# A Trainium2 attention and experts kernel: tiles of x handed back at another place, softplus with ScalarE's exponential, another order of v's loads, and stores issued by ScalarE

## The chip, the core and the metric

The program runs on one core of one Trainium2 chip. A core has five engines with instruction queues of their own: TensorE (PE; its weight loads PEld stand apart in the profile), VectorE (DVE), ScalarE (ACT), GpSimd (POOL) and SyncE (SP). Each runs its queue in order, and they wait for each other through semaphores. The metric is device time in microseconds of one execution, lower is better.

## The reference

Three stages follow one another. Attention over q, k, v of shape (4, 8, 576, 64) adds a local one (a band of 3 positions to either side) and one over means of 4 positions, repeated 4 times. Its output, as x with 2304 rows of 512, goes through a mixture of 8 experts with two experts for each row, and then through one with a single expert for each row.

```python
out = repeat(softmax(q_d @ k_d.T * scale) @ v_d, 4) + softmax(where(|i - j| < 4, q @ k.T * scale, -1e9)) @ v
x = out.transpose(0, 2, 1, 3).reshape(2304, 512)

noisy = x @ w_gate + log1p(exp(x @ w_noise)) * noise
top2, weight = two largest of noisy, softmax over these two
x = sum over the two of weight * relu(x @ w1[e]) @ w2[e]

e = argmax(x @ gate2 + modality_bias[modality_id]),  w = its softmax value
x = w * relu(x @ w1_2[e]) @ w2_2[e]
```

The log1p(exp(.)) over the noise logits is the softplus that the change touches.

## The kernel before

**The attention loop.** Heads go in pairs, 16 of them (4 batches of 4 pairs); two pairs are a group g, whose q, k and v are loaded together. The loop over i from 0 to 17 is software-pipelined. Step i begins with the transposes of q and k of pair i + 1 (`transposes`, tiles pq and pk), finishes the softmax of pair i - 1 (`softmax2`: VectorE's sum sm and reciprocal, then the banded probabilities Pd, three quarters on GpSimd, and the coarse ones ped on GpSimd), and multiplies pair i - 2 with v (`values`, tiles pva and pvm; `scale_d` copies od). Then come the scores of pair i (`scores`, tile pd), the output of pair i - 2 into xT (`combine`), the transposes of pair i - 1's probabilities (`p_transposes`: pp, copied to pT by ScalarE, then ppd, copied to pdT), the first half of pair i's softmax (`softmax1`: mx, pe and an exponential; `softmax_d1` and `softmax_d2`: mxd, ped, smd), and on even steps the rest of the next group (`group`, tile prs). `pool_v` adds four rows of v (vr) into vd on GpSimd, six additions for a group.

**Tiles of x.** x has 18 tiles of 128 rows. `xback_att(t)` multiplies xT of one tile with gw (an identity beside the gates' weights), which gives the rows of x and their logits in one PSUM tile px, from the pool of the scores' tiles (two buffers). Its second half, `rest`, waits in the list `after` until `flush()` is called: ScalarE copies the rows to xr (two buffers), VectorE reduces the logits to lg, and SyncE stores xr to x_rows in HBM. Tiles 0 to 12 are placed in the loop by the tables `before` (ahead of a step's scores) and `behind` (after its coarse transposes); tiles 13 to 17 follow the loop.

**Routing inside the loop.** `route1` is a generator for the routing of the first nine tiles: softplus, the two largest, ranks (`rt.places`, L504 to L507), then 18 pairs of one-hot matrices, oh on VectorE and ol on GpSimd, which TensorE multiplies (`rt.invert`, L551) into a table tab; from it `places_early` makes the indices of the gather. `tick(n)` takes n pieces from it, so that routing instructions stand between those of the softmax; a piece that yields "PE" waits for `unblock`. `route1` is put into `back` in step 12. It is used again for the other nine tiles while the experts run.

**SyncE's queue.** Loads and stores are issued in program order: `load_qk(g + 2)` and `load_vr(g + 1)` in odd steps, `load_vw(g)` in even ones, a store for each tile of x, and in step 14 the first weights (raw) and 5.9 MB of zeros into the rows of the second stage. A DMA whose buffer isn't free holds up all that stand behind it.

**Experts.** After the loop the rows are gathered by indirect DMA (xg), transposed (L729), and multiplied with w1 and w2 split in two parts each (L746, L758), until the end.

## Time and profile before

| | |
|---|---|
| median of 3 runs | 925.9 us (923.14 to 927.91) |
| profiled execution, its own time | 926.93 us |
| its span in the trace | 925.2 us |
| mean granted TensorE clock | 0.973 |
| TensorE busy | 870.4 us (94%), 6775 matmuls |
| VectorE, ScalarE, GpSimd busy | 550.4, 429.0, 322.3 us |
| attention and first routing | 0 to about 178 us |
| first matmul of the experts | 177.83 us |

The busy shares are means over two very different parts: up to about 178 us several engines pass work around in a loop, and behind it TensorE works almost without a gap. The page's slices of the span show both: TensorE has 5 to 9 tenths in the first eight slices, and 9 in nearly all that follow. A timeline row gives the start, the duration, the engine, the line and operation, the names, how many like instructions were merged, and in brackets the idle time of the engine just before, with what ended it. SyncE's rows are the time of issuing a DMA, waits of later merged ones included.

### The profile page before, as it was taken

What the parts mean: (1) busy time and instruction counts of PE and PEld (TensorE: products, weight loads), DVE (VectorE), ACT (ScalarE), POOL (GpSimd) and SP (SyncE); (2) the same over time, 40 slices, a digit from 0 to 9 for tenths busy, and PEclk for the clock granted to TensorE, in tenths of its full rate; (3) what the DMA queues carried; (4) which work ended last, traced back from release to release, by engine and by line L of the source; (5) the groups of instructions that cost most, each with busy time, mean ns of one, the idle gap of its engine ahead of it and who ended that gap; (6) DMA issues with size and microseconds to landing.
All of it is one profiled execution on the core that took longest, in us unless ns stands there. A gap on an engine that the chain in (4) does not pass through costs nothing. (4 is left out here: it accounts for less than half of the span.)

```text
span 925.2 us, 18236 instructions
## 1 busy us (share of the span) xinstructions
PE 870.4 (94%) x6775; PEld 764.1 (83%) x6775; DVE 550.4 (59%) x1345; ACT 429.0 (46%) x947; POOL 322.3 (35%) x460
## 2 busy tenths in 40 slices
PE   5898977799999999999999999989989999999995
PEld 4777866698888988999898999978867889999994
DVE  6775697489975544554343443434666877556662
ACT  3675644455554534444233342334423356455552
POOL 7876658436553213043106032050020442222210
PEclk9998988899999999999999999999989999999998
DMA  8878659747776457476328245175433467546650
GB/s 175 171 159 189 169 143 329 240 167 229 204 235 195 140 146 181 143 204 147 129 71 182 92 92 162 46 161 161 128 99 109 155 239 245 190 154 220 216 209 24
DMA packets 158702, 153.83 MB, mean 166 GB/s; under 512 B 74319, under 2 KB 119887, under 8 KB 158608
## 3 DMA queue, kind: packets, MB, share of 16 engines
q1 hardware_dynamic: 146528, 120.15, 42.2%
q0 software_dynamic: 12080, 32.45, 15.2%
q8 instruction: 56, 0.92, 0.4%
q14 instruction: 38, 0.31, 0.1%
HBM read 124.98 MB, written 27.85 MB: 165 GB/s over the span
## 5 line engine op out<-in xcount | busy, mean ns | idle before, releaser
L746 PE MATMUL ph<-xh,whi 128*128 128x256 f32 (+3 forms) x768 | 238.4, 310 | 2.8 <-DVE wlo L707 2.1
L746 PE MATMUL ph<-xl,whi 128*128 128x256 f32 (+3 forms) x768 | 237.6, 309 | 0.4 <-DVE xl L732 0.3
L746 PE MATMUL ph<-xh,wlo 128*128 128x256 f32 (+3 forms) x768 | 237.6, 309 | 0.1
L758 PE MATMUL y<-whi,hh 128*128 128x512 f32 x472 | 192.2, 407 | 0.1
L758 PE MATMUL y<-wlo,hh 128*128 128x512 f32 x472 | 188.1, 398 | 0.0
L758 PE MATMUL y<-whi,hl 128*128 128x512 f32 x472 | 187.6, 398 | 0.0
L707 DVE TENSOR_TENSOR wlo<-raw,whi 128x512 fp32r<-128x512 f32 x135 | 93.2, 690 | 157.4 <-ACT whi L706 144.9
L706 ACT ACTIVATE whi<-raw 128x512 fp32r<-128x512 f32 x160 | 101.0, 631 | 170.7 <-PE y L758 155.7
L746 PEld LDWEIGHTS ph<-xh,whi 128*128 128x128 f32 x768 | 146.0, 190 | 12.2 <-issue 2.6
L746 PEld LDWEIGHTS ph<-xl,whi 128*128 128x128 f32 x768 | 145.9, 190 | 8.3 <-DVE xl L732 1.0
L748 ACT ACTIVATE hh<-ph 128x256 fp32r<-128x256 f32 (+3 forms) x192 | 83.2, 433 | 142.3 <-PE ph L746 133.0
L746 PEld LDWEIGHTS ph<-xh,wlo 128*128 128x128 f32 x768 | 146.2, 190 | 1.8 <-DVE wlo L707 0.3
L749 DVE SCALAR_TENSOR_TENSOR hl<-ph,hh 128x256 fp32r<-128x256 f32 (+3 forms) x192 | 92.5, 482 | 84.5 <-ACT hh L748 81.0
L1215 POOL DMA_INDIRECT x_rows<-y,idx x35 | 57.4, 1641 | 208.1 <-ACT y L1206 108.2
L709 DVE TENSOR_TENSOR wlo<-raw,whi 128x512 fp32r<-128x512 f32 x160 | 120.6, 754 | 11.9 <-ACT whi L708 10.9
L758 PEld LDWEIGHTS y<-whi,hl 128*128 128x128 f32 x472 | 89.5, 190 | 21.6 <-DVE hl L749 0.4
L758 PEld LDWEIGHTS y<-whi,hh 128*128 128x128 f32 x472 | 90.2, 191 | 13.6 <-DVE y L1208 0.8
L758 PEld LDWEIGHTS y<-wlo,hh 128*128 128x128 f32 x472 | 89.8, 190 | 12.6
L708 ACT ACTIVATE whi<-raw 128x512 fp32r<-128x512 f32 x160 | 98.6, 616 | 0.0
L732 DVE TENSOR_TENSOR xl<-pt,xh 128x512 fp32r<-128x512 f32 x59 | 38.7, 687 | 30.8 <-ACT xh L731 30.6
L271 POOL TENSOR_TENSOR Pd<-pe,sm 32x380 f32<-32x380 f32 (+1 forms) x48 | 42.1, 877 | 42.8 <-ACT kT L198 10.4
L1215 POOL DMA_INDIRECT out_dram<-y,pi x19 | 20.6, 1084 | 100.6 <-ACT y L1206 44.1
(311 smaller groups left out, 1085.5 us busy)
## 6 DMA issues: line engine op xcount, KB each, us to landing
raw<-in_moe_w_dram SPq DMA_DIRECT2D x160, 512.0 KB
x_rows<-zero SPq DMA_DIRECT2D x1, 5934.0 KB
vr<-in_v_dram SPq DMA_DIRECT2D x16, 288.0 KB
x_rows<-xr SPq DMA_DIRECT2D x18, 256.0 KB
x2l<-x_rows SPq DMA_DIRECT2D x18, 256.0 KB
qk<-in_q_dram SPq DMA_DIRECT2D x32, 128.0 KB
qk<-in_k_dram SPq DMA_DIRECT2D x32, 128.0 KB
vw<-in_v_dram SPq DMA_DIRECT2D x24, 128.0 KB
```

The source lines that it names most:

```text
L271: eng.tensor_tensor(Pd[s, :, W * g:W * g + n], pe[s, :, :n], sm[s, :, None].to_broadcast([W, 2 * NB, n]), op=ALU.mult)
L706: nc.scalar.activation(h1, a, AF.Copy)
L707: eng.tensor_tensor(l1, a, h1.bitcast(F32), op=ALU.subtract)
L708: nc.scalar.activation(hi[:, 1], r2[:, half], AF.Copy)
L709: nc.vector.tensor_tensor(lo[:, 1], r2[:, half], hi[:, 1].bitcast(F32), op=ALU.subtract)
L732: nc.vector.tensor_tensor(xl, p, xh.bitcast(F32), op=ALU.subtract)
L746: nc.tensor.matmul(ps, w[a][:, k], x[b][:, k, s], start=(i == 0), stop=(i == 3 * KD - 1))
L748: nc.scalar.activation(hh[:, s], ps, AF.Relu)
L749: nc.vector.scalar_tensor_tensor(hl[:, s], ps, 0.0, hh[:, s].bitcast(F32), op0=ALU.max, op1=ALU.subtract)
L758: nc.tensor.matmul(p, h[a][:, 128 * j:128 * j + 128], w[b], start=(f == 0 and i == 0), stop=(f == self.FB - 1 and i == 2))
L1215: d = nc.gpsimd.indirect_dma_start(out=dst, out_offset=bass.IndirectOffsetOnAxis(ap=ix, axis=0), in_=y, in_offset=None, **kw)
```

## The change

It does four things.

- The tables `before` and `behind` are replaced by `between`: at most one tile between a step's scores and its pp, and where a step has two, the second between pp and ppd. The copy xr and the reduction lg of a tile are then written behind the exponential of pe. `route1` is put into `back` at the end of step 12 instead of behind its values.
- Softplus takes exp from ScalarE, one instruction, in place of a polynomial of fourteen VectorE instructions; the 13 pieces for `tick` in that part become 4.
- `load_vr` is issued ahead of `load_qk`, and `pool_v` adds one half c of v completely in a step (three additions) instead of one or two parts of both halves.
- The store of xr is issued by ScalarE's queue.

```diff
-EXP = [1.0, 1.0000000360960746, 0.4999999535047545, 0.1666642092713234, 0.04166772440021678, 0.00837476549703475,
-       0.0013859289912904367]
@@ pool_v
-    def pool_v(self, g, part):
+    def pool_v(self, g, c):
         vr, vd = self.gt[g]["vr"], self.gt[g]["vd"]
-        for c in range(2):
+        for part in range(3):
             self.nc.gpsimd.tensor_tensor(vd[:, c], vd[:, c] if part else vr[c][:, :, 0], vr[c][:, :, part + 1], op=ALU.add)
@@ softplus
     V.scalar_tensor_tensor(na, z, -1.0, z, op0=A.mult, op1=A.min)
     yield
-    V.tensor_scalar(na, na, -86.0, None, op0=A.max)
-    yield
-    V.tensor_scalar(n, na, 1.4426950408889634, MAGIC, op0=A.mult, op1=A.add)
-    yield
...
-    for k in range(5, 0, -1):
-        V.scalar_tensor_tensor(p, p, EXP[k], r, op0=A.add, op1=A.mult)
-        yield
-    V.scalar_tensor_tensor(p, p, 1.0, ni.bitcast(F32), op0=A.add, op1=A.mult)
-    yield
+    nc.scalar.activation(p, na, AF.Exp)
+    for _ in range(3):
+        yield
@@ xback_att, rest
-                nc.sync.dma_start(x_rows[128 * t:128 * t + 128, :DM], xr.rearrange("p a b c -> p (a b c)"))
+                nc.scalar.dma_start(x_rows[128 * t:128 * t + 128, :DM], xr.rearrange("p a b c -> p (a b c)"))
@@ the loop
-        before = {6: 0, 7: 2, 10: 5, 11: 7, 14: 10, 15: 12}
-        behind = {6: 1, 7: 3, 9: 4, 10: 6, 11: 8, 13: 9, 14: 11}
+        between = {6: [0], 7: [1], 8: [2], 9: [3], 10: [4, 5], 11: [6, 7], 12: [8], 14: [9], 15: [10], 16: [11], 17: [12]}
             if ph == 1:
+                if g + 1 < 2 * B:
+                    att.load_vr(g + 1)
                 if g + 2 < 2 * B:
                     att.load_qk(g + 2)
-                if g + 1 < 2 * B:
-                    att.load_vr(g + 1)
...
             flush()
-            if i == 12:
-                back.append(route1(0, HT, att_bank, nc.vector, nc.gpsimd, hold))
-                back.append(places_early())
             unblock(1)
-            if i in before:
-                xback_att(before[i])
             if 0 < i < NP:
                 att.scores(i)
...
             tick(2)
+            for t in between.get(i, [])[:1]:
+                xback_att(t)
             if 1 <= i <= NP:
                 pt = att.p_transposes(i - 1)
                 next(pt)
             if 0 < i < NP:
                 att.softmax1(i)
+            flush()
+            for t in between.get(i, [])[1:]:
+                xback_att(t)
...
-                for j in ((0, 1), (2,))[ph] if i > 1 else ((), (0, 1, 2))[ph]:
-                    att.pool_v(g, j)
+                for c in ((0,), (1,))[ph] if i > 1 else ((), (0, 1))[ph]:
+                    att.pool_v(g, c)
...
-            if i in behind:
-                xback_att(behind[i])
             if i == 12:
+                flush()
+                back.append(route1(0, HT, att_bank, nc.vector, nc.gpsimd, hold))
+                back.append(places_early())
```

**TensorE's queue, from pp of step 13 to the scores of step 14.** The names are pp and ppd (probabilities), pq and pk (q and k of the next pair), pva and pvm (values), pd (scores) and px (a tile of x). Before:

```order
L285 MATMUL pp<-gw,Pd_116 128x128 x10
L294 MATMUL ppd<-gw,ped 72x72 x8
L971 MATMUL px<-gw,xT 128x144 x4
L195 MATMUL pq<-gw,qk 128x128 x4
L195 MATMUL pk<-gw,qk 128x128 x4
L311 MATMUL pva<-pdT,vd 64x144 x4
L317 MATMUL pva<-pT,vw_114 64x88 x2
L317 MATMUL pvm<-pT,vw_114 64x122 x8
L971 MATMUL px<-gw,xT 128x144 x4
L213 LDWEIGHTS identB
L213 MATMUL pd<-mask,identB 128x190
```

After, from pk to pp of step 14:

```order
L193 MATMUL pk<-gw,qk 128x128 x4
L309 MATMUL pva<-pdT,vd 64x144 x4
L315 MATMUL pva<-pT,vw_114 64x88 x2
L315 MATMUL pvm<-pT,vw_114 64x122 x8
L211 LDWEIGHTS identB
L211 MATMUL pd<-mask,identB 128x190
L211 LDWEIGHTS identB
L211 MATMUL pd<-mask,identB 128x190
L217 MATMUL pd<-kT_107,qT_109 32x38 x40
L222 MATMUL pd<-kd_113,qd_111 72x144 x4
L952 MATMUL px<-gw,xT 128x144 x4
L283 MATMUL pp<-gw,Pd_117 128x128 x10
```

Before, one tile stood between ppd and pq and another between the values and the scores; after, one stands between the scores and the next pp.

**ScalarE's and VectorE's queues at pp of step 12.** pT, pdT and xr are ScalarE's copies; mx, mxd, sm, kd, qd are VectorE's reductions. Before, ScalarE and then VectorE:

```order
L327 ACTIVATE od<-pva 128x144
L987 ACTIVATE xr<-px 128x512
L286 ACTIVATE pT<-pp 128x488 x2
L286 ACTIVATE pT<-pp 128x244
L235 ACTIVATE pe<-pe 128x380
L296 ACTIVATE pdT<-ppd 72x288 x2
```

```order
L988 TENSOR_REDUCE lg<-px 128x16
L42 TENSOR_TENSOR xT<-pva,od 128x88
L351 SCALAR_TENSOR_TENSOR sp_na<-lg 128x72
L42 TENSOR_TENSOR xT<-pvm,od 128x488
L353 TENSOR_SCALAR sp_na<-sp_na 128x72
L355 TENSOR_SCALAR sp_n<-sp_na 128x72
L357 TENSOR_SCALAR sp_n<-sp_n 128x72
L42 TENSOR_REDUCE mx<-pd 128x10
```

After, ScalarE and then VectorE:

```order
L284 ACTIVATE pT<-pp 128x488 x2
L284 ACTIVATE pT<-pp 128x244
L233 ACTIVATE pe<-pe 128x380
L968 ACTIVATE xr<-px 128x512
L970 DMA x_rows<-xr 128x512
L294 ACTIVATE pdT<-ppd 72x288 x2
```

```order
L40 TENSOR_REDUCE mx<-pd 128x10
L40 TENSOR_TENSOR pe<-pd,mx 128x380
L969 TENSOR_REDUCE lg<-px 128x16
L40 TENSOR_REDUCE mxd<-pd 72x4
L40 TENSOR_SCALAR mxd<-mxd 72x4
L40 TENSOR_REDUCE kd_113<-prs 128x2x16
L40 TENSOR_REDUCE qd_111<-prs 128x2x16
L40 TENSOR_REDUCE qd_111<-pq 128x128
L348 SCALAR_TENSOR_TENSOR sp_na<-lg 128x72
```

The copy xr moved from ahead of pT to behind the exponential of pe, with the store behind it in the same queue; lg moved from ahead of xT to between pe and mxd, and the first softplus instruction from there to behind qd.

**GpSimd's queue at the end of the loop.** Pd and ped are those of steps 14 and 15, vd the last sums of v, ol the one-hot matrices. Before:

```order
L545 TENSOR_SCALAR ol<-r_h_225,lclo 128x128 x3
L271 TENSOR_TENSOR Pd_116<-pe,sm 32x10x38 x2
L271 TENSOR_TENSOR Pd_116<-pe,sm 32x10x32
L545 TENSOR_SCALAR ol<-r_h_225,lclo 128x128 x2
L274 TENSOR_TENSOR ped<-ped,smd 72x576
L545 TENSOR_SCALAR ol<-r_h_225,lclo 128x128 x5
L183 TENSOR_TENSOR vd<-vd,vr 72x256 x2
L271 TENSOR_TENSOR Pd_117<-pe,sm 32x10x38 x2
L271 TENSOR_TENSOR Pd_117<-pe,sm 32x10x32
L274 TENSOR_TENSOR ped<-ped,smd 72x576
L545 TENSOR_SCALAR ol<-r_h_225,lclo 128x128 x8
```

After:

```order
L269 TENSOR_TENSOR Pd_116<-pe,sm 32x10x38 x2
L269 TENSOR_TENSOR Pd_116<-pe,sm 32x10x32
L272 TENSOR_TENSOR ped<-ped,smd 72x576
L526 TENSOR_SCALAR ol<-r_h_225,lclo 128x128 x3
L181 TENSOR_TENSOR vd<-vr 72x256
L181 TENSOR_TENSOR vd<-vd,vr 72x256 x2
L526 TENSOR_SCALAR ol<-r_h_225,lclo 128x128 x6
L269 TENSOR_TENSOR Pd_117<-pe,sm 32x10x38 x2
L269 TENSOR_TENSOR Pd_117<-pe,sm 32x10x32
L526 TENSOR_SCALAR ol<-r_h_225,lclo 128x128
L272 TENSOR_TENSOR ped<-ped,smd 72x576
L526 TENSOR_SCALAR ol<-r_h_225,lclo 128x128 x8
```

Before, ten ol stood ahead of the last Pd and eight behind ped; after, nine stand ahead of it, one between Pd and ped, and eight behind.

## Rows read from the trace of the kernel before

**Rows 1.** TensorE's share and clock in two stretches: busy us (x instructions) by engine, PEclk, DMA

```profile
80.00:100.00 20.00, 17.80 (x310) 14.95 (x311) 13.28 (x36) 11.82 (x39) 12.49 (x19) 0.83 0.82 187
180.00:925.00 745.00, 725.67 (x4242) 641.96 (x4242) 423.37 (x984) 331.09 (x633) 199.72 (x266) 0.98 0.54 160
```

**Rows 2.** TensorE's timeline before the experts: start, us, line, out<-in, count, [idle <-releaser]

```profile
166.90 0.24 PE L551 MATMUL rbank<-oh,ol 128*128 128x144 f16 x1 [0.34 <-POOL ol L545]
177.83 1.48 PE L729 MATMUL pt<-gw,xg 128*128 128x128 f32 x8 [3.09 <-DVE lg L988]
```

**Rows 3.** TensorE's timeline, first pp of steps 3 to 6, 8, 9, 13 to 15

```profile
37.83 1.31 PE L285 MATMUL pp<-gw,Pd 128*128 128x128 f32 x10 [1.54 <-POOL Pd L271]
44.99 1.20 PE L285 MATMUL pp<-gw,Pd 128*128 128x128 f32 x9 [0.60 <-POOL Pd L271]
53.39 1.31 PE L285 MATMUL pp<-gw,Pd 128*128 128x128 f32 x10 [1.54 <-POOL Pd L271]
60.94 1.31 PE L285 MATMUL pp<-gw,Pd 128*128 128x128 f32 x10
77.85 1.09 PE L285 MATMUL pp<-gw,Pd 128*128 128x128 f32 x8 [0.81 <-POOL Pd L271]
89.96 1.20 PE L285 MATMUL pp<-gw,Pd 128*128 128x128 f32 x9
128.79 1.35 PE L285 MATMUL pp<-gw,Pd 128*128 128x128 f32 x8 [2.81 <-POOL Pd L271]
142.29 1.31 PE L285 MATMUL pp<-gw,Pd 128*128 128x128 f32 x10
153.59 1.62 PE L285 MATMUL pp<-gw,Pd 128*128 128x128 f32 x9
```

**Rows 4.** Timelines of ScalarE, VectorE and GpSimd in step 3

```profile
39.77 0.53 ACT L235 ACTIVATE pe<-pe 128x380 f32<-128x380 f32 x1
37.85 0.74 DVE L42 TENSOR_REDUCE mxd<-pd 72x4 f32<-72x576 f32 x1
40.38 0.69 DVE L42 TENSOR_REDUCE qd<-pq 128x128 f32<-128x512 f32 x1 [1.35 <-PE pq L195]
42.15 2.78 POOL L271 TENSOR_TENSOR Pd<-pe,sm 32x380 f32<-32x380 f32 x3 [1.78 <-DVE sm L42]
```

**Rows 5.** A tile's matmuls (TensorE's timeline); all stores of tiles (SyncE, line L989: ns min/median/max)

```profile
147.20 1.25 PE L971 MATMUL px<-gw,xT 128*128 128x144 f32 x8
L989 SPq DMA_DIRECT2D x_rows<-xr x18: 320/350/9874, 64.9 to 177.5; - x18
```

**Rows 6.** Timelines of ScalarE and TensorE in step 8

```profile
79.80 0.60 ACT L987 ACTIVATE xr<-px 128x512 f32<-128x512 f32 x1 [4.25 <-DMA x_rows<-xr]
80.92 0.44 PE L285 MATMUL pp<-gw,Pd 128*128 128x128 f32 x2 [1.98 <-ACT pT L286]
```

**Rows 7.** Softplus: VectorE's timeline, its groups from 115.8 to 131, and ScalarE's L1014

```profile
117.00 0.69 DVE L353 TENSOR_SCALAR sp_na<-sp_na 128x72 f32<-128x72 f32 x1
124.21 0.22 DVE L370 SCALAR_TENSOR_TENSOR sp_p<-sp_p,sp_ni 128x72 f32<-128x72 f32 x1
L384 DVE SCALAR_TENSOR_TENSOR sp_p<-sp_p,sp_u 128x72 f32<-128x72 f32 x3 | 2.1, 699 | 0.0
L1014 ACT ACTIVATE qex<-qex x2: 256/260/263, 146.7 to 227.6; 128x72 f32<-128x72 f32 x2
```

**Rows 8.** GpSimd's timeline at the end of the attention

```profile
157.96 2.78 POOL L271 TENSOR_TENSOR Pd<-pe,sm 32x380 f32<-32x380 f32 x3 [0.45 <-DVE sm L42]
161.94 4.91 POOL L545 TENSOR_SCALAR ol<-r_h,lclo 128x128 f16<-128x128 f16 x8
```

**Rows 9.** SyncE's waits up to 180 us: line <- waited for: us in total, times, longest

```profile
SPq L144 <- POOL vd L183: 19.5, 5, 11.4
```

**Rows 10.** SyncE's timeline around the 5.9 MB of zeros

```profile
142.63 0.48 SPq L1181 DMA_DIRECT2D x_rows<-zero  x1
147.66 9.87 SPq L989 DMA_DIRECT2D x_rows<-xr  x1
```

More of the change, by code (lines that the diff above doesn't have):

```diff
@@ L348, in t @@
         return pool.tile([128, 9, E], dt, tag=f"sp_{n}", name=f"sp_{n}")[:, :T]
-    na, n, m, r, p, u, ni = t("na"), t("n"), t("m"), t("r"), t("p"), t("u"), t("ni", I32)
+    na, r, p, u = t("na"), t("r"), t("p"), t("u")
     V.scalar_tensor_tensor(na, z, -1.0, z, op0=A.mult, op1=A.min)
     yield
-    V.tensor_scalar(na, na, -86.0, None, op0=A.max)
-    yield
-    V.tensor_scalar(n, na, 1.4426950408889634, MAGIC, op0=A.mult, op1=A.add)
-    yield
-    V.tensor_scalar(n, n, MAGIC, None, op0=A.subtract)
-    yield
-    V.scalar_tensor_tensor(r, n, -0.693359375, na, op0=A.mult, op1=A.add)
-    V.tensor_scalar(m, n, 127.0, 8388608.0, op0=A.add, op1=A.mult)
-    yield
-    V.scalar_tensor_tensor(r, n, 2.12194440e-4, r, op0=A.mult, op1=A.add)
-    V.tensor_copy(ni, m)
-    yield
-    V.tensor_scalar(p, r, EXP[6], None, op0=A.mult)
-    yield
-    for k in range(5, 0, -1):
-        V.scalar_tensor_tensor(p, p, EXP[k], r, op0=A.add, op1=A.mult)
+    nc.scalar.activation(p, na, AF.Exp)
+    for _ in range(3):
         yield
-    V.scalar_tensor_tensor(p, p, 1.0, ni.bitcast(F32), op0=A.add, op1=A.mult)
-    yield
     V.tensor_scalar(u, p, 2.0, None, op0=A.add)
```

## The prediction

> **What bounds the kernel now.** I read the stretches of time first. From 180 us on TensorE is busy 725.67 of 745 us at a clock of 0.98 [rows 1]: whatever the change does there is covered, and only the moment at which the experts' matmuls begin can move the end. TensorE's rows give that moment: its first transpose of a gathered tile, L729, starts at 177.83, after waiting 3.09 for the last logits [rows 2]. Before it stand five tiles of x in a chain of their own (px, xr, lg, store), which starts when the last routing matmul L551 has ended, at 166.90 + 0.24 = 167.14 [rows 2]. The change leaves those five tiles as they are, so the 177.83 - 167.14 = 10.69 us behind that matmul stay. Call its end E: the time changes by what E changes. (The gather of the first tokens hangs on E as well, and moves with it.)
>
> What sets E is the loop over the 16 pairs of heads. I call T(i) the start of the first transpose of probabilities (pp, L285) in step i; they are listed in [rows 3]. The loop closes through GpSimd's probabilities Pd (2.78 us), TensorE's pp, ScalarE's copies pT and exponential of pe, and VectorE's sum: in step 3 pp starts at 37.83, the exponential at 39.77, VectorE waits 1.35 for pq until 40.38, and Pd starts at 42.15 [rows 3, 4]. A step without a tile of x takes 44.99 - 37.83 = 7.16 us when its number is odd and 53.39 - 44.99 = 8.40 when it is even (it prepares a group of heads) [rows 3].
>
> **Tiles between scores and pp.** A tile is eight matmuls, 1.25 us, one copy xr of 0.60 on ScalarE [rows 5, 6] and a short reduction lg on VectorE. Before an odd step's pp TensorE has waited 1.54 for Pd [rows 3], so the eight matmuls cost nothing there; without that idle time they would cost 1.25. The new cost is a wait. On ScalarE xr now comes behind the three pT and the exponential, and on VectorE lg comes ahead of mxd, qd and sm and needs xr. In step 3 the exponential ends at 39.77 + 0.53 = 40.30; xr would end at 40.9 and lg at 41.1; mxd (0.74, and a scaling of 0.2) would end at 42.0, and the 42.15 - 40.38 = 1.77 from qd to Pd [rows 4] would follow: Pd at 43.75, 1.6 later. Queued behind lg are the running step's mxd, qd, sm and VectorE's share of Pd; GpSimd and then TensorE wait for these. In an even step kd waits for the copies of prs, which lie behind xr and the store's issue: 0.60 + 0.37, so 1.0 more. Bounds: nothing, if lg and mxd fit in the 1.35 for which VectorE waits for pq; and 1.6 + 1.25, if the matmuls aren't covered either.
>
> The steps, then: 6 and 8 at 9.4, 7 and 9 at 8.8. Step 10 has a second tile behind pp whose PSUM bank waits for the first lg: 9.4 + 1.25 + 0.5 = 11.2. Step 11 has two as well, 8.8 + 1.25 = 10.05. Between T(12) and T(13) stands no tile, but tile 8's lg and the first softplus instructions: 9.6. Together 67.25, so T(13) = 60.94 + 67.25 = 128.2, against 128.79. By pieces: steps 6 and 7 took 16.91 and will take 18.2; steps 9 to 12 took 38.83 and will take 39.65 [rows 3], though a stretch of VectorE (below) goes there; step 8 took 12.11 and will take 9.4, for in it xr waited 4.25 for an earlier store to land, which SyncE had issued behind loads, TensorE waited 1.98 for pT behind that [rows 6], and its clock fell, to 0.83 over 80 to 100 [rows 1].
>
> **Softplus.** Fourteen VectorE instructions from 117.00 to 124.43, 5.0 us busy in all, go; one ScalarE exponential of 72 columns comes, 0.26 like its sister L1014 [rows 7]. The second use of softplus lies inside the experts and is covered. The 5.0 us were on the path in steps 12 and 13, where VectorE was busy without a gap. But what is left of softplus starts a step later, since routing is queued at the end of step 12; in step 13 three of its instructions stand directly ahead of mx, and nine of the routing ahead of Pd. In the new order VectorE has 24 instructions from kd to Pd. The stretch from 117.00 to 124.43 held 23, so 0.32 us each; 24 x 0.32 = 7.7, and 1.1 more since three of them are L384 at 0.70 [rows 7]. The kd starts about with pp, so Pd starts 8.8 after T(13) and T(14) comes 2.8 later, 11.6 in all: 139.8; before it came 13.50 later, at 142.29 [rows 3]. For the step behind T(14) I take the 7.16 of step 3, less its 0.60 of waiting for Pd and about 1.2 for pq and pk, of which there are none any more, and add 2.2 for which the values wait for pdT, behind xr and the store, 0.6 for the ranks (L504) and 1.25 for tile 10: 9.4, so T(15) = 149.2, against 153.59.
>
> **The end of the routing.** The eighteen ol on GpSimd come later: one more is left for the time after Pd of step 15. Pd, ped and the last eight ol ran back to back from 157.96 to 161.94 + 4.91 = 166.85, 8.9 us [rows 8]; with one more ol, 0.6, it is 9.5. On VectorE some seven oh and the weights now stand between pe and sm of step 15 (some 16 instructions at 0.32, 5.2 us, behind an lg that ends 3.5 after T(15); at most 1.5 more where GpSimd slows them), so Pd starts 8.7 to 10.2 after T(15), where it was 157.96 - 153.59 = 4.37 [rows 3, 8]. E = T(15) + 18.2 to 19.7. The middle gives E = 168.2, 1.1 later than now. TensorE's own path (a tile in each of steps 16 and 17) ends about as early. So the loop wins 4.4 us by T(15), and the last stretch, which took 13.55, gives back 5.4.
>
> **Order of v's loads, stores on ScalarE.** SyncE stood 19.5 us, in five waits, at L144 for GpSimd's sums of v, with all else behind it [rows 9]. That goes, and with it part of the delay of stores. The new order puts a group's second vr ahead of qk; it waits for sums of the step before, and qk is wanted two steps later, which covers it; without that slack it would show as pq waiting for a DMA. Issuing costs ScalarE time in eleven of the steps; it is in the sums above at 0.37. No row shows a store issued by ScalarE; SyncE's issues of the same transfer took 0.32 to 9.87, median 0.35 [rows 5, 10]. I take the value near the median, since only one row has the long one, and that one is a rival below.
>
> **Sum.** 926.93 (the profiled execution) + 1.1 = 928.0. The profiled execution is 1.0 above the median of the three, so 927.0 on the median's scale, on which the rivals stand too.
>
> **Rivals.**
> *Faster: the tile is free.* If lg finds its place in VectorE's wait for pq and nothing is added to the loop, steps 6 to 12 lose 4 x 1.0 + 3 x 1.6 = 8.8 us, the time is 918.2; half of it gives 922.6. For it: TensorE's waits for Pd, 1.54 and 0.60 in the steps shown [rows 3], are filled by the tiles. Against: xr can't begin before the exponential ends, and in step 3 that is 0.08 before qd starts [rows 4]. Chance 0.22 for over 4.6 us.
>
> *Slower: the store blocks ScalarE.* SyncE's issue of a store at 147.66 lasted 9.87 us; it was the first transfer issued after the 5.9 MB of zeros, which left SyncE at 142.63 [rows 10]. If a transfer from ScalarE waits in the same way, tile 9's or 10's store holds ScalarE up, with pdT, the values, the ranks and the ol behind it. In the new order the zeros leave at about 130 (no store and no wait for GpSimd ahead of them), and 157.53 - 142.63 = 14.9 later, at 145, they are through; tile 9's store is issued at T(14) + 3 = 143, so 2 us late, and up to 9.87 if the zeros leave late. That gives 929.0 to 936.9. It decides when the zeros are still under way at T(14) + 3. Against it stands the median of 0.35: stores issued next to other loads didn't wait [rows 5]. Chance 0.14. The Trainium skill, Perfetto Trace Analysis, section DMA Instruction — HWDGE, says that the block which generates descriptors is shared between sequencers and locked for exclusive use, and that the recorded time includes the wait for the lock; by that rule ScalarE would share the long row's wait, and the time is this rival's.
>
> *Slower: the clock.* TensorE waits about 1.6 us more in an odd step with a tile. In 80 to 100, with one wait of 1.98, the clock was 0.83 on the mean [rows 1, 6]; 17.80 us of work at that cost some 3 us. Two or three such stretches more, beyond what is in the sum, give 933 to 936. Chance 0.12.
>
> *The stores don't land earlier.* If xr still waits for landings with ScalarE issuing, step 8's 2.7 stays: 929.7, inside the forecast's own range.
>
> **How the numbers follow.** A measurement of this kernel tells 0.5%, or 4.6 us, from no change. The forecast with its own bounds (the last stretch 18.2 to 19.7, a step 0.5 either way) covers 922.5 to 931, most of it within 4.6 of 925.9: chance 0.52. Faster by over 0.5%: 0.22. Slower by over 0.5%: 0.26, the two slow rivals. The range that leaves two in ten outside reaches from near the free tile, 919.0, to the upper part of the blocked store, 934.5.
>
> **What would show it.** T(13), T(14), T(15) near 128, 140 and 149 and E near 168, with lg waiting about 1 us for xr in each of eleven steps. Wrong: odd steps with a tile at 7.2 (then faster); an issue on ScalarE of several us, or a clock below 0.9 between 85 and 120 (then slower); pq waiting for qk.

## The result and the profile after

The changed kernel takes 934.7 us (median of 8 runs, 931.78 to 938.45) against 927.1 for the kernel before in 8 runs taken beside them: the ratio is 1.0088, with a 95% interval of 1.0068 to 1.0108. It is slower by 0.9%; 927.0 was predicted, with a range that ended at 934.5. The profiled execution took 934.3 us, its span is 932.5.

From the first pt on little changed: 747.9 us of the span lie behind it, 747.4 in the kernel before. What was lost was lost ahead of it. TensorE's timeline (start, duration, line, out<-in, count, idle time before and what ended it) gives the steps, answering to [rows 3] and [rows 2]:

```profile
60.73 1.26 PE L283 MATMUL pp<-gw,Pd 128*128 128x128 f32 x10
...
97.09 1.31 PE L283 MATMUL pp<-gw,Pd 128*128 128x128 f32 x10
...
108.62 1.26 PE L283 MATMUL pp<-gw,Pd 128*128 128x128 f32 x10
...
120.40 1.26 PE L283 MATMUL pp<-gw,Pd 128*128 128x128 f32 x10
...
129.89 1.31 PE L283 MATMUL pp<-gw,Pd 128*128 128x128 f32 x10 [1.74 <-POOL Pd L269]
...
152.81 1.25 PE L283 MATMUL pp<-gw,Pd 128*128 128x128 f32 x10
...
170.39 0.24 PE L532 MATMUL rbank<-oh,ol 128*128 128x144 f16 x1 [0.22 <-POOL ol L526]
...
184.59 1.97 PE L710 MATMUL pt<-gw,xg 128*128 128x128 f32 x8 [6.17 <-DVE lg L969]
187.24 0.58 PE L727 MATMUL ph<-xh,whi 128*128 128x256 f32 x1 [0.69 <-ACT xh L712]
```

With the words of the prediction, T(6) is 60.73, T(10) 97.09, T(12) 120.40, T(15) 152.81, E = 170.39 + 0.24 = 170.63, and from E to pt it is 13.96, which is called d from here on. The table sets the stretches of every kernel of this study side by side; all are read from the same view of one profiled execution, us. A stretch in which one kernel differs from another can be read down a column.

| kernel | ratio to before, 95% interval | T(6) to T(10) | T(10) to T(12) | T(12) to T(15) | T(15) to E | d |
|---|---|---|---|---|---|---|
| before | 1 | 38.83 | 16.70 | 37.12 | 13.55 | 10.69 |
| before + softplus (e4) | 0.9949, 0.9928 to 0.9970 | 36.97 | 16.70 | 33.26 | 13.43 | 10.98 |
| before + v's order (e6) | 1.0023, 1.0001 to 1.0044 | 35.61 | 16.68 | 36.86 | 15.41 | 10.55 |
| before + stores on ScalarE (e3) | 1.0047, 1.0029 to 1.0065 | 39.38 | 16.62 | 36.97 | 13.83 | 13.88 |
| before + tables and late routing (e5) | 1.0118, 1.0060 to 1.0177 | 35.12 | 21.22 | 31.58 | 25.01 | 8.44 |
| before + softplus + v's order (e8) | 0.9938, 0.9908 to 0.9968 | 35.15 | 16.68 | 30.61 | 15.25 | 10.78 |
| e8 + late routing (e12) | 0.9986, 0.9970 to 1.0001 | 36.07 | 16.69 | 31.50 | 20.84 | 10.49 |
| e8 + four xr (e11) | 0.9863, 0.9841 to 0.9886 | 34.98 | 16.69 | 31.54 | 13.88 | 8.54 |
| **after** | 1.0088, 1.0068 to 1.0108 | 36.36 | 23.31 | 32.41 | 17.82 | 13.96 |
| after, tail stores on SyncE (e1) | 1.0088, 1.0061 to 1.0114 | 36.42 | 25.61 | 32.30 | 17.77 | 10.76 |
| the same again (e10) | 1.0058, 1.0038 to 1.0077 | 36.49 | 25.65 | 32.30 | 17.96 | 10.77 |
| after, all stores on SyncE (e9) | 1.0046, 1.0028 to 1.0065 | 35.13 | 22.83 | 29.70 | 19.65 | 13.80 |
| after, lg ahead of xr (e2) | 1.0085, 1.0061 to 1.0109 | 36.45 | 20.66 | 32.12 | 17.45 | 16.99 |
| e2, xr behind pdT (e7) | 1.0104, 1.0070 to 1.0138 | 35.24 | 23.91 | 31.17 | 21.31 | 16.55 |
| after, four xr (e13) | 1.0050, 1.0029 to 1.0072 | 36.47 | 25.59 | 32.18 | 17.77 | 8.50 |
| after, early routing (e14) | 1.0132, 1.0095 to 1.0170 | 36.44 | 26.64 | 29.50 | 19.26 | 13.93 |
| after, both (e15) | 1.0076, 1.0050 to 1.0102 | 36.43 | 29.04 | 29.49 | 19.36 | 8.76 |
| after, both, stores on SyncE (e16) | 1.0015, 0.9997 to 1.0033 | 35.14 | 26.75 | 29.44 | 19.34 | 8.92 |

One execution of each kernel was profiled, and that limits what a column can tell. Before and e4 issue the same instructions up to T(6), which is 60.94 in the one and 64.03 in the other. Most profiled executions lie within 2.2 us of the median of their kernel; e7's lies 4.1 above it, e6's 3.6 and e14's 4.2 below.

Against before, pt comes 6.76 us later: -0.21 by T(6), -2.47, +6.61, -4.71, +4.27 by the columns, and +3.27 for d. So the change gained 7.4 us, most of it in the steps where SyncE's stalls and the softplus had been, and lost 14.2 in three other places.

**Steps 10 and 11.** These have two tiles each, the second between pp and ppd. TensorE's and VectorE's timelines in step 11:

```profile
111.77 1.51 PE L952 MATMUL px<-gw,xT 128*128 128x144 f32 x8 [1.89 <-DVE lg L969]
```

```profile
111.49 0.23 DVE L969 TENSOR_REDUCE lg<-px 128x16 f32<-128x64 f32 x1 [2.63 <-ACT xr L968]
...
115.13 0.69 DVE L40 TENSOR_REDUCE qd<-pq 128x128 f32<-128x512 f32 x1 [2.56 <-PE pq L193]
```

lg waits for xr, the second px waits 1.89 for lg, ppd and pq stand behind px in TensorE's queue, and VectorE's qd then waits 2.56 for pq. In the kernel before no px waited for an lg in the whole loop.

**The last stretch ahead of pt.** ScalarE's, GpSimd's and SyncE's timelines, from 174 us on:

```profile
176.26 0.60 ACT L968 ACTIVATE xr<-px 128x512 f32<-128x512 f32 x1 [1.77 <-DMA x_rows<-xr]
...
177.90 0.60 ACT L968 ACTIVATE xr<-px 128x512 f32<-128x512 f32 x1 [1.04 <-DMA x_rows<-xr]
...
183.68 0.60 ACT L968 ACTIVATE xr<-px 128x512 f32<-128x512 f32 x1 [5.18 <-DMA x_rows<-xr]
```

```profile
182.31 0.20 POOL L786 COPY meta<-xg 128x16 f32<-128x16 f32 x1 [5.20 <-DMA xg<-x_rows,idx]
```

```profile
174.57 0.37 SPq L675 DMA_DIRECT2D raw<-in_moe_w_dram  x1
174.98 0.51 SPq L676 DMA_DIRECT2D raw<-in_moe_w_dram  x1
```

The last copy xr waits 5.18 for an earlier store to land. SyncE's queue has no stores any more, so the next weights (two loads of 512 KB) leave it at 174.57, ahead of the last stores; before, they stood behind these in the queue and left at 177.92. pt waits 6.17 for the lg behind that xr, in place of 3.09 [rows 2]. That the loads which went ahead are what delays the stores and the gather is argued from this order: no run moves the loads alone.

### The profile page after: what moved, and what is told of

Same layout as the page of the kernel before. It is cut to its first block, busy times and chain, and to the rows that moved or that the text cites. A ratio compares the mean times of both kernels' runs of the same rounds, so it can differ in the third digit from the quotient of the medians.

```text
span 932.5 us, 18171 instructions
## 1 busy us (share of the span) xinstructions
PE 870.5 (93%) x6775; PEld 762.6 (82%) x6775; DVE 541.5 (58%) x1317; ACT 429.4 (46%) x949; POOL 321.0 (34%) x460
## 5 line engine op out<-in xcount | busy, mean ns | idle before, releaser
L690 DVE TENSOR_TENSOR wlo<-raw,whi 128x512 fp32r<-128x512 f32 x160 | 120.1, 751 | 14.7 <-ACT whi L689 13.5
```

The lines of the kernel that those rows point to most:

```text
L690: nc.vector.tensor_tensor(lo[:, 1], r2[:, half], hi[:, 1].bitcast(F32), op=ALU.subtract)
```

## The experiments

The theories, as they came up: (1) the tail's stores land late since SyncE's loads run ahead of them; (2) lg, which waits for xr, lengthens the loop; (3) TensorE's wait for pdT, behind xr and the store on ScalarE, does; (4) the later start of the routing costs the last stretch; (5) the landings act through the two buffers of xr alone.

### Each part alone on the kernel before

Stores issued by ScalarE (e3):

```diff
-                nc.sync.dma_start(x_rows[128 * t:128 * t + 128, :DM], xr.rearrange("p a b c -> p (a b c)"))
+                nc.scalar.dma_start(x_rows[128 * t:128 * t + 128, :DM], xr.rearrange("p a b c -> p (a b c)"))
```

> The kernel before with one edit: all stores of tiles are issued by ScalarE. Theory 1 expects that the wait of 4.25 for a landing in step 8 goes (T(9) about 2.7 earlier), that the weights' loads leave SyncE before the last stores, and that the distance from the last L551 to the first pt grows from 10.7 to about 14: time 926 to 931. Rival (ScalarE's store is the cost): issues of over 1 us on ScalarE, time above 932. Rival (the stores don't matter): 927.

932.6 us, ratio 1.0047, above the 926 to 931 that were expected. d went from 10.69 to 13.88, nearly what it is in the changed kernel, with no other edit made: the stores' queue is the cause of the longer d. Step 8 fell from 12.11 to 10.27, but step 9 rose from 9.81 to 12.28, so the stall that the prediction wanted to win there only moved: no xr waits there any more, but GpSimd's sum of v waits 2.75 for its load, TensorE waits 3.47 for Pd behind that, and the granted clock is 0.50 in the 3.2 us that follow.

```profile
83.48 0.73 POOL L183 TENSOR_TENSOR vd<-vr 72x256 f32<-72x256 f32 x1 [2.75 <-DMA vr<-in_v_dram]
```

```profile
89.83 2.40 PE L285 MATMUL pp<-gw,Pd 128*128 128x128 f32 x10 [3.47 <-POOL Pd L271]
```

This run bears on the rival of the blocked ScalarE too. ScalarE's and SyncE's timelines of e3:

```profile
150.61 0.33 ACTq L989 DMA_DIRECT2D x_rows<-xr  x1
152.06 0.33 ACTq L989 DMA_DIRECT2D x_rows<-xr  x1
```

```profile
140.28 0.94 SPq L1181 DMA_DIRECT2D x_rows<-zero  x1
154.43 2.96 SPq L1030 DMA_DIRECT2D x_rows<-wb  x1
```

The zeros were issued at 140.28. ScalarE issued its stores 10.3 and 11.8 us behind them, in 0.33 us each. In the kernel before SyncE's issue that began 5.0 us behind the zeros lasted until 14.9 us behind them [rows 10], so a wait of that kind would have caught both stores. SyncE's own next issue in e3 began only at 154.43; its 2.96 us are no second case, for the profile puts a wait of 3.6 there down to a store of xr.

Softplus on ScalarE (e4; the diff is that of the change):

> The kernel before with one edit: softplus takes ScalarE's exponential. If VectorE's fourteen instructions, 5.0 us, were on the path in steps 12 and 13, T(14) comes 3 to 5 us earlier and the time falls to 922 to 924. If they were covered by other waits, or the nine pieces of routing that are taken sooner fill the place, it stays within 1.5 of 927.

922.3 us, ratio 0.9949: T(12) to T(15) falls from 37.12 to 33.26, with no other edit made. The tables and the late routing (e5; the diff is that of the change):

> The kernel before with one edit: the tiles of x stand where the change puts them (between the scores and pp, second ones between pp and ppd), with routing queued at the end of step 12; softplus, the order of v and the stores stay as before. Theory 3 (a step with a tile between scores and pp is bound by TensorE's own work, 8.5 and 9.4 us, and a step with two by its second tile's wait, 11.5 and 11.8; the last stretch from T(15) is 4 us longer): T(12) is 2 to 4 us later than in the kernel before, E 5 to 8 us later, time 932 to 936. Rival (the placement itself is free and the loss comes from the stores alone): 925 to 929.

936.4, ratio 1.0118. T(15) comes at 150.22, earlier than before's 153.59, but T(10) to T(12) takes 21.22 instead of 16.70, and T(15) to E 25.01 instead of 13.55. The order of v's loads (e6; the diff is that of the change):

> The kernel before with one edit: the loads of v ahead of those of q and k, and sums of v by halves. Without SyncE's stall at the loads of v (19.5 us in five waits), stores leave earlier and the wait of 4.25 for a landing in step 8 shrinks: time 924 to 927. Rival (loads were far ahead anyway, and the new order delays q and k): 927 to 930, with TensorE's pq waiting for a load.

927.8, ratio 1.0023, interval 1.0001 to 1.0044: the wait of xr for a landing in step 8 falls from 4.25 to 2.13, TensorE's for pT from 1.98 to 0.29, the step takes 9.04, and the time doesn't follow. Together with softplus (e8) the same order goes with 0.9938 instead of 0.9949. Alone it measures 0.2% slower, with softplus 0.1% faster, so nothing beyond the error of the runs is shown for it:

> The kernel before with two edits: ScalarE's exponential in softplus and the new order of v; tiles and stores as before. If the two add, it is 5 below the kernel before for softplus plus what the order of v gives alone: 918 to 922. If the order of v costs, 923 to 926.

Alone, softplus, v's order, the stores and the tables with the late routing change the time by -0.5, +0.2, +0.5 and +1.2%, 1.4% together, where the whole change lost 0.9%. The tables with the late routing are the costliest part.

### The tail

Stores from tile 13 on by SyncE (e1, and once more as e10):

```diff
-                nc.scalar.dma_start(x_rows[128 * t:128 * t + 128, :DM], xr.rearrange("p a b c -> p (a b c)"))
+                (nc.scalar if t < 13 else nc.sync).dma_start(x_rows[128 * t:128 * t + 128, :DM], xr.rearrange("p a b c -> p (a b c)"))
```

> The changed kernel, with the stores of the last five tiles (13 to 17) issued by SyncE again; tiles 0 to 12 stay with ScalarE. Theory 1 (with no stores in SyncE's queue, the next weights' loads run ahead of the last stores and of the gather and delay their landing): L532 still ends near 170.6, the first pt comes about 10.7 us behind it instead of 14.0, and the time falls from 934.7 by about 3.3, to 931.4. Rival (the last five tiles are slow because ScalarE issues them, or because the zeros are still moving): the distance stays near 14 and the time near 934.7.

d was 10.76, as expected, but the time 934.9, ratio 1.0088, no better than the change: in the profiled execution E came later, at 172.98, since step 10 took 13.82 instead of 11.53. The repeat:

> The same kernel as e1 (only the last five stores by SyncE), with more rounds. There the distance behind the last L532 fell by 3.2 us in the trace but the median didn't fall. If the tail counts, the median of more runs lies 2 to 4 below the changed kernel's 934.7; if something takes the gain back (the first experts' loads, now later), the distance is 10.7 again and the median stays at 934 to 936.

Again d 10.77 and step 10 at 13.86; the median was 933.1, ratio 1.0058, 1.5 us below the changed kernel's where 2 to 4 were expected. So the shorter d is seen in both traces and hardly in the medians. All stores by SyncE (e9):

> The changed kernel with all stores of tiles issued by SyncE again. Theory 1 (ScalarE's stores cost in the tail, where loads of weights run ahead of the last stores, and by the issue ahead of pdT in the loop): the first pt comes about 10.7 us behind the last L532 instead of 14.0, steps 7 and 9 lose the 0.4 of the issue, time 929 to 931. Rival (undoing the stores brings back waits for landings that are as long): 933 to 936.

931.2, ratio 1.0046, about as expected, but d was 13.80 and not 10.7: a miss, for another reason. The issue of a store by SyncE at 153.08 took 8.23 us behind the zeros of 147.74; the stores behind it were late, and the first xr of the tail waited 5.96 for one. Without ScalarE's issues steps 6, 8 and 9 took 8.92, 8.98 and 8.64 in place of 9.38, 9.36 and 9.10, and step 7 took 8.59 for 8.52.

Four buffers for xr in the changed kernel (e13):

```diff
-            xr = axr.tile([128, 2, 2, 128], F32, tag="xr", name="xr")
+            xr = axr.tile([128, 2, 2, 128], F32, tag="xr", name="xr", bufs=4)
```

> The changed kernel, with four buffers for xr where it has two; everything else as it is. In the changed kernel the last copies xr wait 1.77, 1.04 and 5.18 us for stores to land, and the way from E to the first pt takes 13.96. Tail theory (late landings reach pt through xr and lg alone): those three waits go, d falls to 8.5 to 9.5 and the time to 929 to 930.5; if the clock falls in step 10 (that step at 13.8 instead of 11.5), 931.5 to 933. Rival (the gather of tokens, whose second part landed at 182.3, holds the experts up by itself): d stays at 12 or more, or another wait of 3 us or more follows pt, and the time stays at 933 to 936.

932.2, ratio 1.0050. No xr of the tail waits, and the first pt hardly does; TensorE's timeline of e13:

```profile
181.43 0.66 PE L710 MATMUL pt<-gw,xg 128*128 128x128 f32 x4 [0.95 <-DVE lg L969]
...
184.09 1.12 PE L710 MATMUL pt<-gw,xg 128*128 128x128 f32 x4 [2.01 <-DMA xg<-x_rows,idx]
...
185.90 0.58 PE L727 MATMUL ph<-xh,whi 128*128 128x256 f32 x1 [0.69 <-ACT xh L712]
```

d is 8.50, so the landings reached the first pt through xr's two buffers. But theory 5 is only two thirds of it: the other half of pt now waits 2.01 for the second gather, which comes late as well. From E to the first ph it is 185.90 - 172.93 = 12.97 us, against 187.24 - 170.63 = 16.61 in the changed kernel: 3.6 won, not 5.5. Of these 2.3 were lost in step 10, which took 13.80 again, so that the span is 1.5 shorter. Two stretches of step 10 of the changed kernel and then of e13 (the length of the stretch, busy us by engine in the order TensorE, its weight loads, VectorE, ScalarE, GpSimd, then PEclk, DMA share and GB/s):

```profile
97.00:104.00 7.00, 5.10 (x50) 4.44 (x50) 3.65 (x10) 4.37 (x16) 3.06 (x4) 1.00 0.76 183
104.00:112.00 8.00, 5.84 (x132) 4.81 (x129) 4.61 (x15) 4.18 (x11) 5.91 (x7) 1.00 0.92 194
```

```profile
97.00:104.00 7.00, 5.10 (x38) 4.35 (x37) 3.17 (x9) 3.78 (x12) 3.28 (x4) 0.85 0.78 193
104.00:112.00 8.00, 8.00 (x140) 6.82 (x139) 5.13 (x15) 3.15 (x12) 5.58 (x7) 0.70 0.89 186
```

Same instructions, same wait of 1.90 ahead of the second px; in e13 the granted clock falls to its lower level (1.2 GHz) behind it, to 0.50 from 102 to 108 us, and sixteen pvm take 1.85 us instead of 1.01. In the changed kernel's profiled execution it fell one step later, to a mean of 0.58 from 112 to 116 us, behind the wait of 1.89. Step 10 took 13.8 to 13.9 in four profiles in which the clock fell behind this wait (e1, e10, e13, e15) and 10.7 to 11.5 in the six others with a second px ahead of ppd, in which it didn't fall there. In e7, with 13.91, it fell later, behind 1.54 us in which TensorE stood still among the scores' last matmuls. Up to tile 13 the changed kernel, e1 and e10 are the same program, so it isn't the edit that makes the difference. What decides it no run here shows, and since one execution of each kernel was profiled, 2 to 3 us of a difference between two of these profiles can be this.

### The loop

lg ahead of xr (e2):

```diff
-                nc.scalar.activation(xr, pv[:, :, :, :128], AF.Copy)
                 nc.vector.tensor_reduce(lg[:, t], pv[:, :, :, 128:].rearrange("p a b c -> p c a b"), axis=AX.XY, op=ALU.add)
+                nc.scalar.activation(xr, pv[:, :, :, :128], AF.Copy)
```

> The changed kernel, with lg written ahead of xr, so that VectorE's lg waits for the tile's matmuls only and ScalarE's xr waits for lg. Theory 2 (VectorE's wait for xr, 1.1 to 2.6 us in each of eleven steps, lies on the loop and costs 1.6 in odd and 1.0 in even steps): steps 7 and 9 fall from 9.36 and 9.10 to about 7.5 and 7.5, the second tiles in steps 10 and 11 start at once instead of 1.9 late, T(15) comes some 10 us earlier (near 143), and the time is 926 to 929, the longer end unchanged. Rival (the step is bound by pq, pdT or the matmuls of the tile, and the wait of lg only hides one of them): T(15) moves by under 3 us and the time stays within 3 of 934.7.

934.8, ratio 1.0085. Steps 6 to 9, with one tile each, stayed at 36.45 (36.36 in the changed kernel): theory 2 falls for them. Steps 10 and 11, where the second px waits for the first tile's readers, fell from 23.31 to 20.66; but the second px still waits, 1.64 for xr, and 1.6 of these 2.65 us are the clock's: TensorE's matmuls of step 11 took 8.28 us at 1.00 in place of 9.89 at 0.86. What was won there was lost in d, 16.99, where pt now waited for an xr.

xr behind pdT in steps with one tile, on top of e2 (e7):

```diff
-            flush()
+            if between.get(i, [])[1:]:
+                flush()
...
                 finish_now(pt)
+            if not between.get(i, [])[1:]:
+                flush()
```

> The changed kernel with lg ahead of xr, as in the run before, and besides xr and its store behind pdT on ScalarE in steps with one tile. Theory 3 (of a single-tile step 0.9 us is TensorE's wait for pdT, which stands behind xr and the store): steps 7 and 9 fall from 8.60 and 9.10 to about 7.7 and 8.2, steps 6 and 8 from 9.37 by up to 1, the second tiles' steps stay at 10.7 and 9.9; time 2 to 4 below 934.8. Rival (TensorE would be waiting for Pd at that point instead): the steps stay within 0.3 of what they were.

936.3, ratio 1.0104, no faster. Steps 7 and 9 fell from 8.60 and 9.10 to 7.99 and 8.57, steps 6 and 8 stayed at 9.37 and 9.31: theory 3 holds for odd steps alone. In an even step another wait takes the place: in step 6 of the changed kernel TensorE waits 0.94 for pdT, and in e7 it waits 0.80 for qd instead. ScalarE's and TensorE's timelines of the changed kernel, then TensorE's of e7, show these waits:

```profile
72.39 0.61 ACT L968 ACTIVATE xr<-px 128x512 f32<-128x512 f32 x1
73.03 0.33 ACTq L970 DMA_DIRECT2D x_rows<-xr  x1
73.41 0.70 ACT L294 ACTIVATE pdT<-ppd 72x288 f32<-72x288 f32 x2 [0.40 <-ACT xr L968]
```

```profile
64.51 0.66 PE L193 MATMUL pk<-gw,qk 128*128 128x128 f32 x4 [0.94 <-ACT pdT L294]
...
73.86 0.76 PE L309 MATMUL pva<-pdT,vd 72*64 72x144 f32 x6 [0.87 <-ACT pdT L294]
...
146.23 0.87 PE L309 MATMUL pva<-pdT,vd 72*64 72x144 f32 x6 [2.63 <-ACT pdT L294]
```

```profile
68.87 1.06 PE L315 MATMUL pvm<-pT,vw 128*64 128x122 f32 x16 [0.80 <-DVE qd L40]
```

### The place of the tiles and the start of the routing

Late routing alone, on e8 (e12):

```diff
-            if i == 12:
-                back.append(route1(0, HT, att_bank, nc.vector, nc.gpsimd, hold))
-                back.append(places_early())
             unblock(1)
...
             if i == 12:
+                flush()
+                back.append(route1(0, HT, att_bank, nc.vector, nc.gpsimd, hold))
+                back.append(places_early())
```

> The kernel of e8 (softplus on ScalarE, order of v) with one more edit: routing is queued at the end of step 12, as in the change, while the tiles stay where they were. Theory 4 (queuing it later moves one-hot matrices into the last steps, and with them E): from T(15) to E 18 to 20 us instead of 15.3, time 2 to 5 above e8. Rival (the last stretch is long because of the tiles' place): unchanged, 918 to 920.

926.3, ratio 0.9986 against e8's 0.9938: by the ratios, each against the kernel before in its own runs, 0.5% or 4.4 us lost, of the 2 to 5 expected. T(15) is the same (145.0 and 144.57), T(15) to E takes 20.84 instead of 15.25: theory 4, in the old placement. In the new one it was undone by itself, with tile 8 put back behind step 11's coarse transposes (e14), and together with four xr (e15):

```diff
-        between = {6: [0], 7: [1], 8: [2], 9: [3], 10: [4, 5], 11: [6, 7], 12: [8], 14: [9], 15: [10], 16: [11], 17: [12]}
+        between = {6: [0], 7: [1], 8: [2], 9: [3], 10: [4, 5], 11: [6, 7], 14: [9], 15: [10], 16: [11], 17: [12]}
...
             flush()
+            if i == 12:
+                back.append(route1(0, HT, att_bank, nc.vector, nc.gpsimd, hold))
+                back.append(places_early())
             unblock(1)
...
+            if i == 11:
+                xback_att(8)
             if i == 12:
-                flush()
-                back.append(route1(0, HT, att_bank, nc.vector, nc.gpsimd, hold))
-                back.append(places_early())
-
```

> The changed kernel, with tile 8 behind the coarse transposes of step 11 and the routing queued at the start of step 12, as in the kernel before; all other tiles keep their new place. Theory 4 (what the new placement costs is the late routing): the last stretch from T(15) to E falls from 17.8 to 12 to 15, steps 12 and 13 may lengthen by 1 to 2 us in all, and the time is 926 to 931. Rival (the place of the tiles costs by itself, and T(13) to T(15) move out by as much as the last stretch wins): 932 to 936.

> Both of the two edits before: four buffers for xr, routing queued at the start of step 12. If they add up: 921 to 926, with d at 8.5 to 9.5 and T(15) to E at 12 to 15. If one of the two is hidden by the other: no better than the better of them, 926 to 930.

938.7 (ratio 1.0132) and 934.0 (1.0076): misses. Steps 12 to 14 win 2.9 us against the changed kernel, but step 11 takes 15.36 instead of 11.78: tile 8, now behind ppd, waits 1.94 for ScalarE's ped, with pq behind it in the queue, and the clock falls. T(15) to E takes 19.26, no less than with late routing, and from T(12) to E 1.5 us are won in all. So in the new placement the start of the routing is not the main cost. The last pair of kernels measures the place of the tiles: e11, e8 with four xr, and e16, which is e15 with the stores on SyncE, so that nothing but the tables is different (`before` and `behind` in e11, `between` in e16).

> The kernel before with softplus on ScalarE, the new order of v, and four buffers for xr instead of two. In the tail xr waited 1.27 and 1.88 us for a store to land so that a buffer came free. Theory 5 (the five tiles' chain is bound by the landing of stores): the distance from the last L551 to the first pt falls from 10.8 to about 8.5, then bound by the gather; time 2 below e8's 918.8, 915 to 918. Rival (bound by the bank of px or by the gather): 918 to 920.

> As the one before, with the stores issued by SyncE again: it differs from the fastest kernel so far (914.2: softplus on ScalarE, new order of v's loads, four buffers) by the place of the tiles alone. If the place of the tiles costs by itself: 917 to 925. If it is neutral: 912 to 916. If it gains: below 912.

e11 takes 914.2 us, ratio 0.9863 (0.9841 to 0.9886), faster than both kernels and than the 915 to 918 expected; its span is 4.6 us shorter than e8's, of which d gives 2.2, and the rest isn't accounted for. e16 takes 928.3, ratio 1.0015. The place of the tiles costs 14.1 us, more than was expected of the costliest case. By the table 10.1 of them come from T(10) to T(12) and 5.5 from T(15) to E. TensorE's timeline of e11 in step 10 and then of e16 in steps 10 and 11, and VectorE's and GpSimd's of e16 in step 11:

```profile
97.31 1.31 PE L285 MATMUL pp<-gw,Pd 128*128 128x128 f32 x10
98.46 0.68 PE L294 MATMUL ppd<-gw,ped 72*72 72x72 f32 x8
...
99.55 1.25 PE L954 MATMUL px<-gw,xT 128*128 128x144 f32 x8
100.64 0.60 PE L195 MATMUL pq<-gw,qk 128*128 128x128 f32 x4
...
103.24 1.25 PE L954 MATMUL px<-gw,xT 128*128 128x144 f32 x8
...
106.07 1.31 PE L285 MATMUL pp<-gw,Pd 128*128 128x128 f32 x10
```

```profile
97.22 1.31 PE L283 MATMUL pp<-gw,Pd 128*128 128x128 f32 x10
100.48 1.25 PE L952 MATMUL px<-gw,xT 128*128 128x144 f32 x8 [1.96 <-DVE lg L969]
101.57 0.67 PE L292 MATMUL ppd<-gw,ped 72*72 72x72 f32 x8
...
102.55 0.66 PE L193 MATMUL pq<-gw,qk 128*128 128x128 f32 x4
...
107.61 1.25 PE L952 MATMUL px<-gw,xT 128*128 128x144 f32 x8
...
115.70 2.29 PE L952 MATMUL px<-gw,xT 128*128 128x144 f32 x8 [2.04 <-ACT ped L251]
```

```profile
118.88 0.69 DVE L40 TENSOR_REDUCE qd<-pq 128x128 f32<-128x512 f32 x1 [6.17 <-PE pq L193]
```

```profile
120.66 2.77 POOL L269 TENSOR_TENSOR Pd<-pe,sm 32x380 f32<-32x380 f32 x3 [9.07 <-DVE smd L40]
```

Both have two tiles between the pp of step 10 and that of step 11. In e11 they stand behind ppd and ahead of the scores, and TensorE waits for neither: 8.76 us. In e16 one stands between pp and ppd and waits 1.96 for an lg that waits for xr: 11.47. Step 11 isn't like for like: up to the next pp e16 has tiles 7 and 8 in it and e11 only 8. Tile 7 waits 1.96 as in step 10, tile 8 waits 2.04 for ScalarE's ped, the clock is at 0.50 from 114 to 120 us, and all of it reaches pq, qd and Pd: 15.28, against 7.93 in e11.

## Why the prediction was wrong

**What bounds the kernel: right.** The kernels of the table end 744 to 750 us behind pt, while pt lies anywhere from 167.96 (e11) to 192.03 (e7). **"The 10.69 us stay": wrong, and the largest miss, +3.27.** The five tiles' code is unchanged, but their stores moved to another queue, and with that the order in which the loads of weights and the stores leave. I had asked what else stands in the queue that the stores join, not what may now leave earlier from the one that they left. e3 shows 3.2 us with this edit alone, e13 takes 3.6 of the way from E to the first ph away by buffers. The rows showed both facts that were needed: the last store is issued at 177.5 [rows 5], and pt comes at 177.83 [rows 2].

**Steps 6 to 9: the size right, the reason wrong.** 36.4 was predicted, 36.36 measured. But lg's wait for xr, which the sum was built on, doesn't set it: e2 takes it away and the steps stay. In odd steps half a microsecond is TensorE's wait for pdT (e7), and in steps 6, 8 and 9 some 0.4 each is ScalarE's issue of the store (e9), which the sum had at 0.37 in even steps; what sets the rest isn't taken apart. That the sum came out right is luck: the mechanism behind it was another. The wait of lg itself is there and longer than the predicted 1 us. The waits of VectorE in the changed kernel, those of the tail included (line <- waited for: us in total, times, longest):

```profile
DVE lg L969 <- ACT xr L968: 29.9, 13, 5.6
```

**Steps 10 and 11: the term was too small, 21.25 for 23.31.** Step 10 was near, 11.2 for 11.53. Step 11 was priced with the second tile's matmuls alone, 10.05, and took 11.78. The wait for the first lg that I counted in step 10 holds there too, 1.89, but it isn't the greater part: e5 has the same tiles and the same wait of 1.96 in step 11, its clock stays at 1.00, and the step takes 10.30; in the changed kernel the clock is 0.86 over the step. TensorE's timeline of e5 in step 11, and then the changed kernel's:

```profile
111.61 1.25 PE L971 MATMUL px<-gw,xT 128*128 128x144 f32 x8 [1.96 <-DVE lg L988]
...
113.19 0.60 PE L195 MATMUL pq<-gw,qk 128*128 128x128 f32 x4
...
117.56 1.25 PE L971 MATMUL px<-gw,xT 128*128 128x144 f32 x8
```

```profile
114.03 1.06 PE L193 MATMUL pq<-gw,qk 128*128 128x128 f32 x4
...
119.32 1.25 PE L952 MATMUL px<-gw,xT 128*128 128x144 f32 x8
```

From one px to the other it is 5.95 us in e5 and 7.55 here: of the 1.73 missed in step 11, about 1.5 go with the clock, which the sum had at its upper level. At that level the price of the tables in these two steps was right, 21.22 in e5. Against the old place it is +6.61 where +4.55 was predicted.

**Steps 12 to 14: 32.41 for 30.6.** T(13) to T(14) was 11.59, predicted 11.6. Step 14 was 11.33 for 9.4: the values waited 2.63 for pdT (above) where 2.2 was taken, and behind that the clock was at 0.67 on the mean from 145 to 150 us. In e9 the same step took 9.51 with the clock at 1.00 and a wait of 1.83; TensorE was busy 7.23 us in it and 8.50 in the changed kernel, so 1.3 of the 1.9 go with the clock here too.

**The last stretch: 17.82, just below the lower bound of 18.2.** The late routing lies in it, as e12 shows for the old placement (5.6 us more), but e14 shows that taking it back alone wins nothing in this stretch once the tiles stand between scores and pp. What sets it there stays open.

**Softplus: right. SyncE's stalls: in part.** Softplus alone is worth 0.5% (e4). The waits at v's loads were to go, and went from 19.5 us in total [rows 9] to 13.9 in three; no xr in step 8 waits, but neither the order of v's loads (e6) nor the stores' queue (e3) gains time alone. **The rival of the blocked store: wrong.** All eighteen issues on ScalarE were short, which answers to SyncE's 320/350/9874 ns [rows 5]:

```profile
L970 ACTq DMA_DIRECT2D x_rows<-xr x18: 326/327/386, 63.7 to 184.3; - x18
```

The prediction had set beside it the section DMA Instruction — HWDGE of the Trainium skill's Perfetto Trace Analysis. It names VectorE's and SyncE's sequencers as those that share the block, with a note that which two engines issue such transfers is the compiler's choice, and I had carried it over to ScalarE. In the changed kernel the zeros left at 131.63 and tile 9's store at 145.12, 13.5 us behind them, which hardly puts the rival to the test. In e3 ScalarE issued in 0.33 at a distance behind the zeros at which SyncE was still held up in the kernel before, so ScalarE doesn't share that wait in these runs.

**The clock.** The sum had taken the upper level in steps 11 and 14, where it fell (0.86 and 0.85 over the step), and about 2.8 us of the misses go with that. The rival that named the clock is not confirmed by it: from T(6) to T(15) the mean is 0.94, where the kernel before has 0.91, with falls in steps 8, 13 and 14 where here they are in 11, 13 and 14, and from 85 to 120 us it is 0.95, above the 0.9 that was to be its sign. The measured time lies in the ranges of both slow rivals, without the mechanism of either.

The chances had 0.52 for no change within 0.5%; the sum of the four misses (d, steps 10 and 11, steps 12 to 14, the last stretch), 3.27 + 2.06 + 1.81 - 1.18 = 5.96, is the distance between 928.0 and 934.3 but for 0.3. The step of the prediction that failed first is that the 10.69 us behind E stay: they became 13.96, and the stores' new queue is what changed them (e3; e1 and e10 take it back).

## What to carry to other kernels

When a transfer is moved to another queue, ask also what the old queue will now issue earlier. A late store shows where its buffer is next written, and more buffers (from two to four xr: ratio 0.9863 in place of 0.9938 here) were worth more than another issuer (1.0047). Extra work that borrows the PSUM buffers of a loop belongs where nothing of the loop's own chain stands behind its wait in any in-order queue: in step 10 two tiles behind ppd and ahead of the scores took 8.76 us (e11), against 8.40 for an even step without a tile [rows 3], and with one of them ahead of ppd and the other behind the scores it took 10.92 at the same clock (e5, e9). And parts of a change that are worth 0.5% each should be run apart: softplus, the new order of loads and two more buffers, without the rest, gain 1.4% where the whole change lost 0.9%.

## What was not expected of the hardware

Where SyncE's next issue followed the 5.9 MB of zeros by 4 to 8 us, it lasted 6.5 to 10.1 us (9.87 before, 8.23 in e9, 6.50 in e6, 10.09 in e11) and ended 13.6 to 15.0 us behind the issue of the zeros, while ScalarE's issues stayed at 0.33. TensorE's clock fell behind one wait of 1.9 us in some executions and not in others of the same instructions, at a price of some 2 to 3 us in that step.
